# Start addresses of TensorE's operands: pads of 64 and 192 bytes

## The chip, the cores and the metric

The kernel runs on one NeuronCore of one Trainium2 chip. The core has TensorE (matrix products), VectorE (called DVE in the profile), ScalarE (ACT), GpSimd (POOL) and SyncE (SP, here only a queue that issues transfers). They share one on-chip memory of 128 partitions. A matrix product takes its two operands from that memory, one of them stationary (it is loaded into the array first, in the profile as PEld) and one moving (it streams past), and leaves its result in an accumulator memory. The metric is the device time of one execution in microseconds, lower is better.

## The reference

Four sequences of 3008 rows of 256 values go through a spectral layer and then, row by row, through a two-layer network:

```
X  = rfft(x, axis=1)                      # along the sequence
Yr = Xr @ w_r - Xi @ w_i + b_r            # complex 256 x 256 mix
Yi = Xr @ w_i + Xi @ w_r + b_i
Y  = soft-threshold(Yr, Yi; 0.01)
y  = irfft(Y, n=3008, axis=1)             # 12032 rows of 256
h  = y @ w_in                             # 256 -> 2048
out = (h * sigmoid(h)) @ w_out            # 2048 -> 256
```

All of it is float32.

## The kernel before

**The arithmetic.** The transforms are done as matrix products with tables (3008 = 47 x 64), in two stages forward (s1, s2), a mix per pair of frequencies, and two stages back (i1, i2). The network takes the result in 24 blocks of 512 rows. Most products are made of float32 values split into a high and a low part, each in the faster one-pass format (fp32r): three matmuls, high by high, high by low and low by high, add up in one accumulator. Such a matmul has 128 stationary columns and 256 moving ones. In this text it is called a split product. A few products are plain float32, which the array does in two passes, and they show as two records in the trace: the second forward stage (L344, L410), the last inverse stage (L544, L551), and parts of the first stage in the opening.

**The lines that matter.**

- L375 and L435: the mix of the first sequence and of the other three. Moving: the mix weights wr, wi, ws. Stationary: xh and xl.
- L482: the third stage, moving zh, zl; stationary the table t3.
- L620 (`mlp1`): the first layer for blocks 0 to 9 and the last. Moving: the block xt0 (high part), xt1 (low part). Stationary: the weights win0, win1. Twelve matmuls in a row a piece.
- L706 (`fast_product`): the first layer for blocks 10 to 22, in a form with seven products in place of eight. Moving: xt0, xt1 or sums made of them, th, tl. Stationary: win0, win1 or sums of them, sw_h0 to sw_h7 and sw_l0 to sw_l7.
- L777 (`mlp2`): the second layer. Moving: wout, high and low part 1024 bytes apart. Stationary: gh, gl, the activations.
- L551 and L544 (`i2`, `i2_ends`): they make the next block's 512 columns, in three pieces a block: `i2` with e = 0, `i2` with e = 1, and `i2_ends` (written "i2e" in the rows).

**What sets the order.** The order is written out by hand. A list of ticks, 16 for a block, says which twelve or so matmuls of the first layer run; between them stand the second-layer products of the tick before, and a table `fill` drops one piece of the spectral work into a tick. From tick 160 on (blocks 10 to 22, about 713 to 1277 us) the spectral work is over, and a tick holds only L706, L777 and, in three ticks of sixteen, a piece of L551 or L544.

**What sets the addresses.** Tiles lie in pools, each a stack in every partition, in the order in which they are asked for: cst at the bottom (tables, win, wout), then sb (the blocks xt, the tiles g, gh, gl, gin), then tf (all of the spectral work). When the spectral work ends, tf is given up and tl takes its place (th, tl, sw_h, sw_l, new gh and gl). A pad is a tile of [128, 16] float32 that nothing uses, which moves all tiles that come after it in its pool, and the pools above it, by 64 bytes:

```
    def shift(pool):

        state["shifts"] += 1
        pool.tile([128, 16], F32, bufs=1, name=f"shift{state['shifts']}")
```

There are seven pads: one in cst ahead of wout, one in sb, two in tf, and three in tl.

Of the kernel before, what the change touches and what calls it, by code (L numbers as in the profile page):

```python
# [9 lines left out]
F32 = mybir.dt.float32  # L10
F32R = mybir.dt.float32r
# [138 lines left out]
def spectral_mlp_kernel(ctx: ExitStack, tc: tile.TileContext, x, w_r, w_i, b_r, b_i, w_in, w_out, c1, c2, c3, c4, c3f, c5, out):  # L150
    nc = tc.nc
    cst = ctx.enter_context(tc.tile_pool(name="cst", bufs=1))
    sb = ctx.enter_context(tc.tile_pool(name="sb", bufs=2))
    tf = tc.alloc_tile_pool(name="tf", bufs=1)
    ps = ctx.enter_context(tc.tile_pool(name="ps", bufs=1, space=PSUM))
    dr = ctx.enter_context(tc.tile_pool(name="dr", bufs=1, space=DRAM))

    def shift(pool):

        state["shifts"] += 1  # L160
        pool.tile([128, 16], F32, bufs=1, name=f"shift{state['shifts']}")

    state = {"prologue": True, "fast": False, "d": 0, "xy": 0, "w": 0, "shifts": 0}
    c1_sb = tf.tile([128, 96], F32, name="c1_sb")
    c1_hl = [tf.tile([128, 96], F32R, name=f"c1_{i}") for i in range(2)]
    x_sb = [tf.tile([128, 4 * D], F32, name=f"x_sb{i}") for i in range(2)]
    c4_sb = cst.tile([120, 2 * (NP + RR)], F32, name="c4_sb")
    bias = tf.tile([128, 2, D], F32, name="bias")
# [1 line left out]
    wi = [tf.tile([128, 2, D], F32R, name=f"wi{i}") for i in range(2)]  # L170
    ws = [tf.tile([128, 2, D], F32R, name=f"ws{i}") for i in range(2)]
    win = [cst.tile([128, 2, DFF], F32R, name=f"win{i}") for i in range(2)]
    shift(cst)
    wout = cst.tile([128, NFF, 2, D], F32R, name="wout")
    scr1 = [dr.tile([NR, 128, D], F32, name=f"scr1_{b}") for b in range(NB)]
    scr2 = [dr.tile([NR, 128, D], F32, name=f"scr2_{b}") for b in range(NB)]

    tl = None
# [485 lines left out]
    def fast_moving(i):  # L664

        x32 = xf.pop(i)
        first = i == FAST[0]
        if first:
            shift(tl)
        d = tl.tile([128, 4, HB], F32, tag="td", bufs=1, name="td")  # L670
        hi = tl.tile([128, 4, HB], F32R, tag="th", bufs=2, name="th")
        lo = tl.tile([128, 4, HB], F32R, tag="tl", bufs=2, name="tl")
        if first:
            shift(tl)
        th[i] = (hi, lo)
        l0, r0, l1, r1 = x32[:, 0, 0:HB], x32[:, 0, HB:BLK], x32[:, 1, 0:HB], x32[:, 1, HB:BLK]

        def low(k):
            nc.gpsimd.tensor_sub(lo[:, k, :], d[:, k, :], hi[:, k, :])

        nc.gpsimd.tensor_sub(d[:, 0, :], r0, l0)
        yield
        nc.gpsimd.tensor_sub(d[:, 1, :], r1, d[:, 0, :])
        yield
        nc.gpsimd.tensor_sub(d[:, 2, :], r1, r0)
        nc.scalar.copy(hi[:, 0:2, :], d[:, 0:2, :])
        yield
        low(0)
        yield
        nc.gpsimd.tensor_sub(d[:, 3, :], l1, d[:, 1, :])  # L690
        yield
        low(1)
        nc.scalar.copy(hi[:, 2:4, :], d[:, 2:4, :])
        yield
        low(2)
        yield
        low(3)
# [160 lines left out]
    with tc.manual_schedule():  # L858
# [2 lines left out]
        nc.scalar.activation(out=first, in_=first, func=ACTF.Silu)  # L861
        zero = tf.tile([128, 512], F32, tag="c", bufs=1, name="zero")
        x_sb.append(tf.tile([128, 4 * D], F32, tag="sx", bufs=1, name="x_sb2"))
        shift(tf)
        c5_sb = tf.tile([128, 128], F32R, name="c5_sb")
        x_pre.extend(x_sb)
        x_pre.extend(sb.tile([128, 4 * D], F32, tag=f"xt{k}", bufs=1, name="x_pre") for k in ("a0", "a1", "b0", "b1"))
        shift(sb)
        nc.sync.dma_start(out=c1_sb, in_=c1)
        nc.gpsimd.memset(zero, 0.0)  # L870
        for n, t in enumerate(x_pre):
# [43 lines left out]
        def w_go(n=1):  # L915

            for _ in range(n):
                if w_run:
                    v = w_run[0]
                    v[0] += 1  # L920
                    if next(v[1], 0) == 0:
                        w_run.pop(0)
                    if v[0] == 2:
                        w_begin()
# [75 lines left out]
        g_load(0, 1, cols=slice(2 * D, 4 * D))  # L1000
        s1(1, 4, late=True)
        w_go()
        shift(tf)
        w_tags[:] = [(("zl", 2), ("zh", 2))]
        s1(1, 5, late=True)
        flush(2)
# [105 lines left out]
        for i in range(FAST[0], len(BLOCKS)):  # L1112
            if i in FAST:
                first = max(16 * i - 13, last + 1)
                t = last_stage(i, first)
                moving = fast_moving(i)
                for k in range(8):
                    at(t + 1 + (k if first == 16 * i - 13 else k // 2), next, moving, None)
                assert t + 8 < 16 * i or first > 16 * i - 13
            else:  # L1120
                last_stage(i, 16 * i - 7)

        def swap_pools():
            nonlocal tl
            tf.release()
            tl = ctx.enter_context(tc.tile_pool(name="tl", bufs=1, reuse_waits="tile"))
            shift(tl)

        fill.setdefault(last + 1, []).insert(0, (swap_pools, ()))
        for q in range(NFF // 2):  # L1130
            steps = fast_weights(q)
# [20 lines left out]
        for t in range(len(ticks) + 1):  # L1152
            i, f = ticks[t] if t < len(ticks) else (LAST, None)
# [38 lines left out]
        for k, (dst, src) in enumerate(stores):  # L1192
            eng = nc.scalar if k % 2 else nc.sync
            n = dst.shape[0]
# [27 lines left out]
```

## Time and profile before

| | |
|---|---|
| median of three runs | 1319.85 us (1319.2 to 1321.52) |
| the profiled execution, its own time | 1320.44 us |
| its span, first to last instruction | 1318.4 us |
| PE busy | 1305.7 us (99% of the span) |
| DVE, ACT, POOL busy | 902.6, 794.6, 196.8 us |
| mean granted TensorE clock | 0.999 of full speed |

PE is busy from the first products to the end. A matmul's record lasts longer than the distance to the next one, since matmuls overlap; what PE's work costs is read from the distance between the starts of two neighbours, called a step here. The timeline view merges equal neighbours into one row ("x12"), so the mean step of a group is the next row's start less its own, over the count.

### The profile page before, as it was taken

The numbers are of one execution on the slowest core, as the hardware profiler recorded it, in microseconds if no ns is written. First come the engines' busy times: TensorE is split into PE (matmuls) and PEld (weight loads), VectorE is DVE, ScalarE is ACT, GpSimd is POOL, SyncE is SP. The second block draws the span as 40 slices with busy tenths as digits, with TensorE's granted clock in tenths as the row PEclk, the third lists the DMA queues.
The fourth block names the chain that finished last, engine by engine and source line by source line (L and its number), as shares of the span: only waits on it lengthen the run. The fifth ranks groups of instructions, "written<-read, shape, count | busy, mean of one in ns | idle before, by whom it ended". The sixth has DMA issues, their size and how long they took to land.

```text
span 1318.4 us, 27508 instructions
## 1 busy us (share of the span) xinstructions
PE 1305.7 (99%) x10869; PEld 1279.3 (97%) x10869; DVE 902.6 (68%) x1723; ACT 794.6 (60%) x1664; POOL 196.8 (15%) x296
## 2 busy tenths in 40 slices
PE   8999999999999999999999999999999999999998
PEld 3989999999999999999999999999999999999998
DVE  3777747877767787566659666667666666666663
ACT  5556555767667666545555666656656665665554
POOL 2001002222122221121102110111011101100100
PEclk9999999999999999999999999999999999999999
DMA  8886324554365443433210111001001110110000
GB/s 267 269 250 192 115 64 116 130 152 104 108 183 138 122 137 82 134 94 111 69 62 12 38 32 32 6 28 32 23 8 40 33 32 2 32 32 16 2 23 25
DMA packets 76168, 110.30 MB, mean 84 GB/s; under 512 B 8880, under 2 KB 54824, under 8 KB 76040
## 3 DMA queue, kind: packets, MB, share of 16 engines
q1 hardware_dynamic: 61921, 79.17, 20.2%
q0 software_dynamic: 10544, 25.68, 7.7%
q10 hardware_dynamic: 3575, 3.70, 0.9%
q8 instruction: 86, 1.41, 0.4%
q14 instruction: 42, 0.34, 0.1%
HBM read 71.03 MB, written 37.49 MB: 82 GB/s over the span
## 4 chain that ended last, share of the span: by engine, by line
PE 96%; DMA 1%; DVE 1%; ACT 1%; issue 0%; POOL 0%; SPq 0%; DVEq 0%; ACTq 0%
PE acc L777 39%; PE h L706 19%; PE h L620 17%; PE mix L435 6%; PE mix L375 3%; PE s L410 2%; PE i L482 2%; PE i L551 2%; PE i2e L551 2%; PE s L304 1%; PE s L344 1%; DMA scr<-s1o 1%; PE s L266 1%; PE i L479 1%; PE i L544 1%; PE warm L886 0%
## 5 line engine op out<-in xcount | busy, mean ns | idle before, releaser
L777 PE MATMUL acc<-wout,gh 128*128 128x256 f32 x3008 | 550.5, 280 | 0.0
L777 PEld LDWEIGHTS acc<-wout,gh 128*128 128x128 f32 x3008 | 459.6, 188 | 3.5 <-issue 0.5
L777 PE MATMUL acc<-wout,gl 128*128 128x256 f32 x1504 | 419.2, 279 | 0.8 <-DVE gl L637 0.8
L777 PEld LDWEIGHTS acc<-wout,gl 128*128 128x128 f32 x1504 | 282.2, 188 | 1.4 <-DVE gl L637 1.4
L620 PE MATMUL h<-xt,win 128*128 128x256 f32 x2016 | 261.7, 278 | 0.4 <-ACT xt L579 0.3
L620 PEld LDWEIGHTS h<-xt,win 128*128 128x128 f32 x2016 | 243.8, 188 | 0.8 <-ACT xt L579 0.5
L627 ACT ACTIVATE g<-h 128x512 f32<-128x512 f32 (+1 forms) x177 | 101.8, 576 | 130.5 <-PE h L620 128.9
L754 DVE TENSOR_TENSOR gl<-gp,gh 128x512 fp32r<-128x512 f32 x208 | 148.5, 714 | 26.0 <-ACT gh L753 26.0
L744 ACT ACTIVATE gp<-gp 128x256 f32<-128x256 f32 x104 | 43.5, 418 | 177.0 <-DVE gp L741 177.0
L637 DVE TENSOR_TENSOR gl<-g,gh 128x512 fp32r<-128x512 f32 (+1 forms) x177 | 116.9, 661 | 47.7 <-ACT gh L636 46.0
L753 ACT CAST gh<-gp 128x512 fp32r<-128x512 f32 x208 | 129.0, 620 | 6.6
L706 PE MATMUL h<-xt,win 128*128 128x256 f32 x624 | 107.0, 279 | 0.0
L636 ACT CAST gh<-g 128x512 fp32r<-128x512 f32 (+1 forms) x177 | 106.2, 600 | 1.1 <-PE acc L777 0.3
L746 DVE TENSOR_TENSOR gp<-h,u 128x256 f32<-128x256 f32 x104 | 44.1, 424 | 78.6 <-ACT gp L745 78.6
L454 DVE TENSOR_TENSOR y<-q,mix 64x256 f32<-64x256 f32 x144 | 60.3, 419 | 45.0 <-PE mix L435 37.0
L706 PE MATMUL h<-th,sw_h 128*128 128x256 f32 x312 | 90.5, 290 | 0.0
L706 PEld LDWEIGHTS h<-xt,win 128*128 128x128 f32 x624 | 88.0, 188 | 0.0
L706 PE MATMUL h<-th,sw_l 128*128 128x256 f32 x312 | 87.1, 279 | 0.0
L706 PE MATMUL h<-tl,sw_h 128*128 128x256 f32 x312 | 86.7, 278 | 0.0
L741 DVE TENSOR_TENSOR gp<-h,u 128x256 f32<-128x256 f32 x104 | 44.1, 424 | 56.9 <-PE h L706 56.5
L442 POOL TENSOR_TENSOR q<-q,bias 128x256 f32<-128x256 f32 x36 | 29.0, 805 | 350.8 <-ACT q L441 350.8
L752 ACT ACTIVATE gp<-gp 128x512 f32<-128x512 f32 x104 | 66.1, 635 | 0.0
(167 smaller groups left out, 2333.9 us busy)
## 6 DMA issues: line engine op xcount, KB each, us to landing
a<-scr SPq DMA_DIRECT2D x48, 256.0 KB
x_sb<-in_x_dram POOLq DMA_DIRECT2D x64, 188.0 KB, 3.7
gin<-scr SPq DMA_DIRECT2D x48, 192.0 KB
t<-in_c_dram POOLq DMA_DIRECT2D x36, 256.0 KB, 3.6
scr<-i1o SPq DMA_DIRECT2D x36, 256.0 KB
t<-in_c_dram SPq DMA_DIRECT2D x48, 128.0 KB
scr<-s1o SPq DMA_DIRECT2D x32, 192.0 KB
scr<-s1o SPq DMA_DIRECT2D x13, 384.0 KB
```

What stands on the lines that cost most here:

```text
L435: nc.tensor.matmul(out=out, lhsT=x_[:, e, c, :], rhs=m[:, e, :], start=(n == 0), stop=(n == 5))
L454: nc.vector.tensor_tensor(out=y[64 * i:64 * i + 64, r, :], in0=q[rows, i, :], in1=pv[rows, i, :], op=op,)
L551: nc.tensor.matmul(out=p[:, o:o + NP + RR], lhsT=t[:, q:q + 128], rhs=c4_sb[:, h * (NP + RR):(h + 1) * (NP + RR)], start=(h == 0), stop=(h ...
L620: nc.tensor.matmul(out=p[:, c:c + D], lhsT=w[:, e, f * 128:(f + 1) * 128], rhs=v[:, e, c:c + D], start=(m == 0), stop=(m == 5),)
L627: nc.scalar.activation(out=g[:, q], in_=p[:, q], func=ACTF.Silu)
L636: nc.scalar.copy(gh[:, q], g[:, q])
L637: nc.vector.tensor_sub(gl[:, q], g[:, q], gh[:, q])
L706: nc.tensor.matmul(out=p, lhsT=w[j], rhs=m[k], start=(begins and n == 0), stop=(n == 2), skip_group_check=True,)
L752: nc.scalar.activation(out=v, in_=v, func=ACTF.Silu)
L753: nc.scalar.copy(h, v)
L754: nc.vector.tensor_sub(l, v, h)
L777: nc.tensor.matmul(out=a[:, 0:D], lhsT=v[:, q], rhs=wout[:, f, w, :], start=(begins and m == 0), stop=(ends and m == 2),)
```

## The change

`shift` gets the number of bytes as an argument. The pads in cst and sb stay at 64 bytes, one in tf stays at 64 and one (ahead of the tiles zl, zh) becomes 192; in tl the first stays at 64, the one ahead of td, th, tl becomes 192, the one behind them stays at 64. The small table c1, in two parts, gets its high part in cst, where it fills 384 bytes ahead of wout.

```
-    def shift(pool):
+    def shift(pool, n):
 
         state["shifts"] += 1
-        pool.tile([128, 16], F32, bufs=1, name=f"shift{state['shifts']}")
+        pool.tile([128, n // 4], F32, bufs=1, name=f"shift{state['shifts']}")
...
-    c1_hl = [tf.tile([128, 96], F32R, name=f"c1_{i}") for i in range(2)]
+    c1_lo = tf.tile([128, 96], F32R, name="c1_lo")
...
     win = [cst.tile([128, 2, DFF], F32R, name=f"win{i}") for i in range(2)]
-    shift(cst)
+    c1_hl = [cst.tile([128, 96], F32R, name="c1_hi"), c1_lo]
+    shift(cst, 64)
     wout = cst.tile([128, NFF, 2, D], F32R, name="wout")
...
         if first:
-            shift(tl)
+            shift(tl, 192)
         d = tl.tile([128, 4, HB], F32, tag="td", bufs=1, name="td")
         hi = tl.tile([128, 4, HB], F32R, tag="th", bufs=2, name="th")
         lo = tl.tile([128, 4, HB], F32R, tag="tl", bufs=2, name="tl")
         if first:
-            shift(tl)
+            shift(tl, 64)
...
-        shift(tf)
+        shift(tf, 64)
         c5_sb = tf.tile([128, 128], F32R, name="c5_sb")
...
-        shift(sb)
+        shift(sb, 64)
...
         w_go()
-        shift(tf)
+        shift(tf, 192)
         w_tags[:] = [(("zl", 2), ("zh", 2))]
...
             tl = ctx.enter_context(tc.tile_pool(name="tl", bufs=1, reuse_waits="tile"))
-            shift(tl)
+            shift(tl, 64)
```

The instructions of all five engines and their order stay as they are. Besides the addresses only some ten of the waits at the swap of tf for tl differ, as the new tiles lie over other old ones. Where the operands of the matmuls begin, modulo 256 bytes, before and after (every column slice that a matmul takes begins at a multiple of 256 bytes from its tile's start, but for the second half of c4):

| line | matmuls | moving | stationary |
|---|---|---|---|
| L375, L435 mix | 936 | 192, stays | 0, stays |
| L482 | 216 | 64 to 192 | 0, stays |
| L620 | 2016 | 64 to 192 | 0, stays |
| L706, moving xt | 819 | 64 to 192 | 0, stays |
| L706, moving xt, with sw_h0 to sw_l2 | 117 | 64 to 192 | 128 to 0 |
| L706, moving th or tl | 897 | 192, stays | 0, stays |
| L706, moving th or tl, with sw_h0 to sw_l2 | 351 | 192, stays | 128 to 0 |
| L777, blocks 10 to 22 (gh, gl in tl) | 2496 | 64 to 192 | 0, stays |
| L777, other blocks (gh, gl in sb) | 2016 | 64 to 192 | 128 to 0 |
| L304, 512 columns | 64 | 192, stays | 0, stays |
| L410, L344, two passes | 192 | 0, stays | 0, stays |
| L551, L544, two passes | 212 | 128 or 180, stay | 128 to 0 |

After the change every split product of 256 columns has 192 moving and 0 stationary.

## Rows read from the trace of the kernel before

**Rows 1.** The profile's page: span, and busy us (share) of the engines.

```profile
span 1318.4 us, 27508 instructions
PE 1305.7 (99%) x10869; PEld 1279.3 (97%) x10869; DVE 902.6 (68%) x1723; ACT 794.6 (60%) x1664; POOL 196.8 (15%) x296
```

**Rows 2.** Windows view: length; busy PE, PEld, DVE, ACT, POOL; PE clock; DMA.

```profile
720.00:1275.00 555.00, 555.00 (x4725) 555.00 (x4724) 376.64 (x780) 337.94 (x762) 72.55 (x96) 1.00 0.09 25
100.00:700.00 600.00, 599.07 (x5112) 594.28 (x5113) 429.07 (x762) 370.47 (x724) 112.64 (x178) 1.00 0.41 116
```

**Rows 3.** Windows view, counts by line: L777, L706, L551; then L777, L620, L435.

```profile
720.00:1275.00 555.00, 331.76 (x2403) 1.00 0.09 25
720.00:1275.00 555.00, 298.33 (x2106) 1.00 0.09 25
720.00:1275.00 555.00, 28.39 (x192) 25.32 (x192) 1.00 0.09 25
100.00:700.00 600.00, 238.64 (x1839) 1.00 0.41 116
100.00:700.00 600.00, 241.39 (x1869) 1.00 0.41 116
100.00:700.00 600.00, 82.28 (x648) 78.71 (x648) 1.00 0.41 116
```

**Rows 4.** Timeline of PE, 382 to 388 us: start, duration, engine, line.

```profile
382.30 0.40 PE L435 MATMUL mix<-wr,xh 128*128 128x256 f32 x2
...
384.43 0.40 PE L777 MATMUL acc<-wout,gh 128*128 128x256 f32 x2
...
385.81 1.52 PE L620 MATMUL h<-xt,win 128*128 128x256 f32 x12
387.17 0.63 PE L304 MATMUL s<-sx,c_sb 111*128 111x512 f32 x2
```

**Rows 5.** Timeline of PE, 1002 to 1005 us, blocks 10 to 22.

```profile
1002.49 0.40 PE L777 MATMUL acc<-wout,gh 128*128 128x256 f32 x2
...
1003.90 0.28 PE L706 MATMUL h<-th,sw_h 128*128 128x256 f32 x1
...
1004.25 0.28 PE L706 MATMUL h<-th,sw_h 128*128 128x256 f32 x1
...
1004.59 0.40 PE L777 MATMUL acc<-wout,gh 128*128 128x256 f32 x2
```

**Rows 6.** Timeline of PE, 35 to 38 us: L375 of the first pair.

```profile
35.59 0.39 PE L375 MATMUL mix<-wr,xh 128*128 128x256 f32 x2
...
37.63 0.60 PE L344 MATMUL s<-t,a 128*128 128x128 f32 x4
```

**Rows 7.** Timeline of PE, 390 to 395 us, behind L410.

```profile
390.37 1.05 PE L410 MATMUL s<-t,a 128*128 128x128 f32 x8
...
392.68 1.57 PE L620 MATMUL h<-xt,win 128*128 128x256 f32 x12
394.09 0.39 PE L777 MATMUL acc<-wout,gh 128*128 128x256 f32 x2
```

**Rows 8.** Timeline of PE: one block's three pieces of L551, then the next's.

```profile
808.42 0.65 PE L551 MATMUL i<-c_sb,gin 120*128 120x141 f32 x4
814.19 0.65 PE L551 MATMUL i<-c_sb,gin 120*128 120x141 f32 x4
819.98 1.13 PE L551 MATMUL i2e<-c_sb,gin 120*128 120x141 f32 x8
820.85 0.38 PE L706 MATMUL h<-th,sw_h 128*128 128x256 f32 x1
852.62 1.13 PE L551 MATMUL i<-c_sb,gin 120*128 120x141 f32 x8
```

**Rows 9.** Lines view, one fifth matmul behind i2e, then behind i2.

```profile
L706 PE MATMUL h<-th,sw_l 128*128 128x256 f32 x1 | 0.3, 276 | 0.0
L706 PE MATMUL h<-th,sw_l 128*128 128x256 f32 x1 | 0.3, 281 | 0.0
```

## The prediction

> **What bounds the kernel now.** I read the page's head first: PE is busy for 1305.7 of 1318.4 us, the next engine, DVE, for 902.6 [rows 1]. Then the windows view for the two long stages. In blocks 10 to 22 (720 to 1275 us) PE is busy for all of 555.00 us, with DVE at 376.64 and ACT at 337.94; in the spectral stage (100 to 700 us) for 599.07 of 600, with DVE at 429.07. The column behind them, the granted clock, is 1.00 in both [rows 2]. So PE sets the time, no engine behind it is near its own limit, and the clock does not explain differences in PE's pace. What is left is the step from one matmul to the next.
>
> The timeline shows two steps for one and the same form of matmul. Twelve L620 take 387.17 - 385.81 = 1.36 us, 113.3 ns each; just ahead, eighteen L435 take 384.43 - 382.30 = 2.13 us, 118.3 ns each [rows 4]. In blocks 10 to 22 twelve L777 take 1003.90 - 1002.49 = 1.41 us, 117.5 ns [rows 5]. L620 itself, fast at 385.81, takes 394.09 - 392.68 = 1.41 us for twelve, 117.5 ns, at another place [rows 7]. There is no third pace: 113.3 and about 118 ns, some 4.5 ns apart. Which one a run of matmuls has is decided at its head and then stays. That is what the change can act on: it alters no instruction, only where operands begin.
>
> **How much is there.** In 720 to 1275 us stand 2403 + 2106 = 4509 split products [rows 3]. The 192 records of L551 come in groups of 8; one lasts 820.85 - 819.98 = 0.87 us [rows 8], and I add 0.09 for the slow first step behind it: 24 x 0.96 = 23 us. L544's few and their changeovers I put at 3. (555 - 26) / 4509 = 117.3 ns a step: this stage runs at the slow pace nearly throughout. At 113.3 it would save 4509 x 4.0 = 18.0 us.
> In 100 to 700 us stand 1839 + 1869 + 648 split products [rows 3] and 216 of L482, 4572. The two-pass products and L304 I put at 70 us, from groups like the eight L410 that begin at 390.37 and L551's [rows 7, 8]. (600 - 70) / 4572 = 115.9 ns: a mixture of both paces, with at most 2.6 x 4572 = 12 us to be had. The opening and the last 40 us hold another 1 us. The ceiling of the change is so 18 + 12 + 1 = 31 us.
>
> **What decides the pace.** I sorted the timeline's steps by the starts in the table of the change, as the distance of stationary from moving modulo 256.
>
> - Distance 192 (64 and 0, or 192 and 128): whatever pace comes in stays. L620 keeps it for twelve matmuls at either pace [rows 4, 7].
> - Distance 64 (64 and 128, or 192 and 0): the slow pace often ends within five steps. L706 with 192 and 0 takes 1004.25 - 1003.90 = 0.35 us for its first three matmuls and 1004.59 - 1004.25 = 0.34 for the next, which is 113.3 ns [rows 5]. I found no run at this distance that went from fast to slow while the starts stayed the same, but for two or three steps in more than a thousand.
> - A switch of the starts between neighbours throws the pace over. The L620 that ends at 382.30 is fast, and L435 behind it (moving from 64 to 192) is slow from its first step; L706 has just become fast at 1004.59, and L777 behind it (192 to 64) is slow again [rows 4, 5]. In blocks 10 to 22 such a switch comes every six to twelve matmuls, between L777 or xt (64) and th, tl (192): this is why the stage is slow.
>
> After the change all split products have 192 and 0, at distance 64, and no switch is left between them. What remains are the changes to and from two-pass products. Then the pace should be set behind each of these, and stay until the next.
>
> The Trainium skill speaks against this. "TensorE: Matmul & The Clock Gate", Part 2 (What happens when you issue a matmul), first step, says that the moving operand and the weight load have two independent read ports, so that loading the next weights takes nothing from the running matmul. By that rule the starts of the two could not matter to each other, and the sum would be zero. The trace doesn't agree: one form runs at 113.3 and at 118 ns at the same granted clock [rows 2, 4, 7].
>
> **The sum, blocks 10 to 22.** A block has three pieces of L551 or L544. In the one shown they begin at 808.42, 814.19 and 819.98, and the next block's at 852.62 [rows 8]: stretches of 5.8, 5.8 and 32.6 us of 44.2.
> - Behind the third (i2e) comes L706 with 192 and 0 already now, and the fifth matmul lasts 276 ns, the mark of the fast pace, against 281 behind the second piece [rows 9]. So it is in all 12 blocks of this stage. Today L777 ends it six matmuls later. I take this stretch as fast.
> - Behind the second, also 192 and 0 now, 4 of 12 become fast. I take it as slow for two thirds.
> - Behind the first stands 192 and 128 now, so no row shows the new case. Bounds: all fast, all slow; I take half.
> Slow: (5.8 x 0.67 + 5.8 x 0.5) / 44.2 = 15%. The gain is 18.0 x 0.85 = 15.3 us; with the first and second piece fast 18, and with the third slow too 0 or less.
>
> **The sum, the spectral stage.** Two edits pull against each other. Switches that begin a stretch at 118 ns go: L435 takes over L620's pace (648 x 4.6 = 3.0 us if always fast; that 192 and 0 in the mix can be fast is shown by L375 at 35.59, eighteen in 2.04 us, 113.3 ns [rows 6]). But switches that end such a stretch go too. Behind L410 L777 starts slow, L620 stays slow until 394.09, where the next switch makes L777 fast [rows 7]. This is so behind nearly all 36 groups of L410, and without a switch it would last to the next two-pass or L304 product. The first edit is worth 3 us by its own count and the second about as much with the sign turned (36 stretches, two pieces longer each, 24 steps of 4.5 ns, are 4 us). I take 0, with bounds +10 (all slow: 4572 x 2.1) and -12 (all fast).
>
> **The other edits** cost nothing that a row shows: the two-pass products' stationary tiles move from 128 to 0, c1's high part into cst, and transfers land 384 bytes further on. Fifteen matmuls of L243 stand in the opening, behind transfers. I take 0, bounded by 1 us either way, the whole of the opening's excess. What PE's pace asks of the others: DVE's 376.64 us in a stage of 540 instead of 555 is 70%, less than the 72% it has in the spectral stage [rows 2], so no new wait of size.
>
> Together: 1320.44 - 15.3 = 1305.1 us for an execution like the profiled one; the median of the runs lies 0.6 below that one, so 1304.5.
>
> **Rivals.**
> 1. *192 and 0 locks the slow pace.* L435 stands at just these starts and never becomes fast in eighteen matmuls [rows 4]; behind L410 the same distance locks too [rows 7]. If this held behind i2e also, once gh and wout follow L706, every step would be 118: 4509 x 0.7 = 3 us more in blocks 10 to 22, 10 us more in the spectral stage, together 1333. It decides from the point where more than nine tenths of blocks 10 to 22 stay slow. Against it: the fifth matmul behind i2e, and L375's eighteen matmuls at 113.3 ns with the same starts [rows 6, 9]. 12%.
> 2. *The starts are not the cause.* The pace would then follow from something that goes with the stage, such as the form of the loop or the engines' writes, and the change would only shuffle it: 1319.9, give or take 1. The Trainium skill's rule on the two ports, above, would have it so. Against it: L706 becomes fast and slow within one tick as its starts go from 64 to 192 and back [rows 5]. 9%.
> 3. *All fast.* If the first and second piece behave like i2e, and the entries of the spectral stage too, the ceiling is reached: 1320 - 31 = 1289. Half of it in the spectral stage gives 1295. It is the forecast's lower edge; 14%.
>
> **How the numbers follow.** The forecast (blocks 10 to 22 mostly fast, the spectral stage between -9 and +6) has 65%; with it and the third rival, faster has 0.79. Rival 1 gives slower, 0.12. Rival 2 gives no change, 0.09; about 0.2% is what a measurement of this kernel can tell from none. The range reaches from 1293, where the forecast meets the third rival, to 1318, a gain of 2 us, where blocks 10 to 22 gain a third of the ceiling and the spectral stage loses 4. It leaves out rival 1, rival 2 and the far end of rival 3.
>
> **What would show it.** Right: behind i2e, L777 and L706 at 113.3 ns for the whole 32 us, so that the 4509 split products fill about 511 us instead of 529; L435 as fast as the L620 ahead of it; 276 ns, the mark of the fast pace, as the duration of most L777 there. Stretches at 118 ns begin at a two-pass or L304 product and nowhere else. Wrong: L777 still at 118 behind L706, a switch of pace where the starts stay the same, or a new idle time of PE in front of gl or gh.

## The result, and the profile after

| | before | after |
|---|---|---|
| median, both run again on one chip | 1320.68 us (1319.2 to 1323.96, 4 runs) | 1308.72 us (1308.18 to 1309.91, 4 runs) |
| ratio | 1 | 0.9907, 95% interval 0.9887 to 0.9928 |
| span of the profiled execution | 1318.4 us | 1306.3 us |

The change makes the kernel 12.0 us faster; 1304.5 was predicted, with a range of 1293 to 1318. Lines behind L172 have numbers one higher than before: L778 is L777 of before, L707 is L706, L621 is L620, L436 is L435, L411 is L410, L552 is L551.

The page's head after answers to [rows 1]: PE is still busy 99% of the span.

```profile
span 1306.3 us, 27506 instructions
PE 1292.0 (99%) x10869; PEld 1264.1 (97%) x10869; DVE 897.0 (69%) x1723; ACT 795.5 (61%) x1664; POOL 196.8 (15%) x296
```

The windows view of the stretches of [rows 2] (window and length; busy PE and matmuls; granted clock, DMA share, GB/s):

```profile
100.00:700.00 600.00, 598.78 (x5082) 1.00 0.42 115
720.00:1275.00 555.00, 555.00 (x4854) 1.00 0.09 25
```

Equal windows hold another number of matmuls: in blocks 10 to 22, 4854 instead of 4725, in the spectral stage 5082 instead of 5112. One stage gained, the other lost, at the same granted clock of 1.00.

The timeline at the L777 and L706 of [rows 5], now:

```profile
998.81 0.39 PE L778 MATMUL acc<-wout,gh 128*128 128x256 f32 x2
...
1000.17 0.28 PE L707 MATMUL h<-th,sw_h 128*128 128x256 f32 x1
...
1000.51 0.28 PE L707 MATMUL h<-th,sw_h 128*128 128x256 f32 x1
...
1000.85 0.39 PE L778 MATMUL acc<-wout,gh 128*128 128x256 f32 x2
```

Twelve L778 take 1.36 us, 113.3 ns each (117.5 before), and six L707 behind them 0.68, the same. The place of [rows 4], now:

```profile
385.45 0.39 PE L436 MATMUL mix<-wr,xh 128*128 128x256 f32 x2
...
387.49 0.39 PE L778 MATMUL acc<-wout,gh 128*128 128x256 f32 x2
...
388.85 1.52 PE L621 MATMUL h<-xt,win 128*128 128x256 f32 x12
390.21 0.40 PE L305 MATMUL s<-sx,c_sb 111*128 111x512 f32 x1
```

Eighteen L436 take 2.04 us: 113.3 ns, as the L621 ahead of them. The other face of it, at 570 us of the spectral stage, behind an L411 as in [rows 7]:

```profile
569.85 1.05 PE L411 MATMUL s<-t,a 128*128 128x128 f32 x8
...
572.15 1.58 PE L621 MATMUL h<-xt,win 128*128 128x256 f32 x12
573.56 0.40 PE L436 MATMUL mix<-wr,xh 128*128 128x256 f32 x2
...
575.68 0.40 PE L778 MATMUL acc<-wout,gh 128*128 128x256 f32 x2
...
577.10 1.58 PE L621 MATMUL h<-xt,win 128*128 128x256 f32 x12
578.51 0.50 PE L411 MATMUL s<-t,a 128*128 128x128 f32 x3
```

From 572.15 to 578.51 stand 54 products in 6.36 us, 117.8 ns each, through three changes of line, up to the next L411. With the same starts everywhere nothing ends a stretch that began badly.

Blocks 10 to 22: the three pieces of the block of [rows 8], as the two-pass products and what follows them.

```profile
810.63 0.38 PE L707 MATMUL h<-th,sw_h 128*128 128x256 f32 x1
...
814.61 0.40 PE L778 MATMUL acc<-wout,gh 128*128 128x256 f32 x2
...
816.03 0.65 PE L552 MATMUL i<-c_sb,gin 120*128 120x141 f32 x4
816.42 0.38 PE L707 MATMUL h<-th,sw_h 128*128 128x256 f32 x1
...
817.21 0.39 PE L778 MATMUL acc<-wout,gh 128*128 128x256 f32 x2
...
817.89 0.28 PE L707 MATMUL h<-xt,sw_h 128*128 128x256 f32 x1
...
821.63 1.13 PE L552 MATMUL i2e<-c_sb,gin 120*128 120x141 f32 x8
822.50 0.38 PE L707 MATMUL h<-th,sw_h 128*128 128x256 f32 x1
...
823.98 0.28 PE L707 MATMUL h<-xt,sw_h 128*128 128x256 f32 x1
...
825.00 0.39 PE L778 MATMUL acc<-wout,gh 128*128 128x256 f32 x2
```

The first piece stays at 118 to its end (twelve L778 from 814.61 to 816.03: 118.3 ns). The second is at 113.3 from 817.21 on (six in 0.68), the third likewise (nine from 823.98 to 825.00 in 1.02). Sorting all 39 stretches between two-pass products by the step of each matmul: the first piece is at 118 throughout in 8 of the 12 blocks, the second in none, the third in 1 of 12 (at 735.4, 31 us). Behind the fifth matmul of a stretch the pace stays to its end, but where PE pauses. In the first of the 39 it does so twice: behind a step of 518 ns at 716.9 us, a wait for gl, the pace is 113 as before it; behind one of 219 ns at 721.7 us it is 118. So a pause too can set the pace anew. In the whole kernel 148 of 151 stretches are at one pace behind their fifth matmul, and the other three hold pauses.

All kernels here issue the same 10869 matmuls in the same order, so their profiled executions, one of each kernel, can be cut at the same matmuls. "Opening" ends at the start of the 601st, blocks 10 to 22 reach from the first L706 to the last; us:

| kernel | opening | spectral | blocks 10 to 22 | rest |
|---|---|---|---|---|
| before | 108.4 | 604.5 | 573.6 | 31.9 |
| after | 108.0 | 608.1 | 558.4 | 31.8 |
| e1_undo_th | 108.2 | 608.6 | 575.3 | 32.7 |
| e2_far192 | 107.5 | 606.4 | 573.4 | 31.7 |
| e3_one_pad | 106.8 | 604.7 | 557.1 | 31.7 |
| e4_mix64 | 111.1 | 602.1 | 556.9 | 31.5 |
| e5_win128 | 107.1 | 604.9 | 556.8 | 31.6 |
| e6_low64 | 109.5 | 618.5 | 573.6 | 32.5 |
| e7_same0 | 107.7 | 624.3 | 585.2 | 33.1 |
| e8_opp128 | 110.4 | 613.4 | 581.2 | 32.3 |
| e9_gl0 | 108.1 | 600.8 | 556.6 | 31.3 |

So the 12.1 us of the span are 15.2 gained in blocks 10 to 22, 3.6 lost in the spectral stage, and 0.5 elsewhere. The opening, which waits for transfers, lies between 106.8 and 111.1 us in these single executions; whether the starts have a part in that, the runs don't show.

### The profile page after: what moved, and what is told of

Its sections match the earlier page's. It is cut to its first block, busy times and chain, and to the rows that moved or that the text cites. A ratio compares the mean times of both kernels' runs of the same rounds, so it can differ in the third digit from the quotient of the medians.

```text
span 1306.3 us, 27506 instructions
## 1 busy us (share of the span) xinstructions
PE 1292.0 (99%) x10869; PEld 1264.1 (97%) x10869; DVE 897.0 (69%) x1723; ACT 795.5 (61%) x1664; POOL 196.8 (15%) x296
## 3 DMA queue, kind: packets, MB, share of 16 engines
q8 instruction: 86, 1.41, 0.4%
## 4 chain that ended last, share of the span: by engine, by line
PE 93%; DMA 3%; DVE 2%; ACT 1%; issue 0%; POOL 0%; SPq 0%; ACTq 0%; DVEq 0%
PE acc L778 39%; PE h L707 19%; PE h L621 17%; PE mix L436 6%; PE s L411 2%; PE i L483 2%; PE mix L376 2%; PE i L552 2%; PE i2e L552 1%; PE s L305 1%; DMA scr<-s1o 1%; PE s L267 1%; PE i L480 1%; PE s L345 1%; DMA t3f<-in_c3f_dram 1%; PE i L545 1%
## 5 line engine op out<-in xcount | busy, mean ns | idle before, releaser
L778 PE MATMUL acc<-wout,gh 128*128 128x256 f32 x3008 | 543.6, 278 | 0.0
L778 PEld LDWEIGHTS acc<-wout,gh 128*128 128x128 f32 x3008 | 458.2, 188 | 3.5 <-issue 1.0
L778 PE MATMUL acc<-wout,gl 128*128 128x256 f32 x1504 | 417.7, 278 | 0.9 <-DVE gl L638 0.9
L778 PEld LDWEIGHTS acc<-wout,gl 128*128 128x128 f32 x1504 | 282.7, 188 | 1.5 <-DVE gl L638 1.5
L621 PE MATMUL h<-xt,win 128*128 128x256 f32 x2016 | 264.5, 280 | 0.4 <-ACT xt L580 0.3
L621 PEld LDWEIGHTS h<-xt,win 128*128 128x128 f32 x2016 | 246.3, 188 | 0.8 <-ACT xt L580 0.5
L707 PE MATMUL h<-xt,win 128*128 128x256 f32 x624 | 105.0, 277 | 0.0
L707 PE MATMUL h<-th,sw_h 128*128 128x256 f32 x312 | 90.1, 289 | 0.0
L707 PE MATMUL h<-th,sw_l 128*128 128x256 f32 x312 | 86.6, 277 | 0.0
L707 PEld LDWEIGHTS h<-xt,win 128*128 128x128 f32 x624 | 86.5, 188 | 0.0
L707 PE MATMUL h<-tl,sw_h 128*128 128x256 f32 x312 | 86.4, 277 | 0.0
```

The lines of the kernel that those rows point to most:

```text
L621: nc.tensor.matmul(out=p[:, c:c + D], lhsT=w[:, e, f * 128:(f + 1) * 128], rhs=v[:, e, c:c + D], start=(m == 0), stop=(m == 5),)
L707: nc.tensor.matmul(out=p, lhsT=w[j], rhs=m[k], start=(begins and n == 0), stop=(n == 2), skip_group_check=True,)
L778: nc.tensor.matmul(out=a[:, 0:D], lhsT=v[:, q], rhs=wout[:, f, w, :], start=(begins and m == 0), stop=(ends and m == 2),)
```

## The experiments

Starts are written moving/stationary, modulo 256; "distance" is stationary minus moving, also modulo 256. All edits are widths of pads (one of 0 bytes is left out) or places of tiles; the work is complete in each kernel.

**e1_undo_th: the whole change, but th and tl keep another moving start than the rest.** Against after:

```
         if first:
-            shift(tl, 192)
+            shift(tl, 64)
         d = tl.tile([128, 4, HB], F32, tag="td", bufs=1, name="td")
...
         if first:
-            shift(tl, 64)
+            shift(tl, 192)
```

> The changed kernel with one part undone: th and tl begin at 64 in place of 192 (the pad ahead of them 64, the one behind 192); all else as after the change (wout, xt at 192, stationary at 0). Theory A (a switch of the moving start between neighbours throws the pace to 118 ns, and with no switch it stays): blocks 10 to 22 hold a switch every six to twelve matmuls again, their 4509 split products go back to 117 ns or more, and the time is 1308.7 + 15 = about 1323 us. Theory B (only the distance of 64 between the starts of neighbours counts, each matmul for itself): the 3261 products with 192 and 0 stay at 113.3 to 114 ns, only the 1248 with th and tl go to 118, and the time is 1308.7 + 5 = about 1313 us. Theory C (starts are not the cause): no change, 1308.7.

Measured 1326.23 us (1324.44 to 1327.48, 6 runs), ratio to before 1.0036 (1.0024 to 1.0048). The timeline where L778 (192/0) meets L707 with th (64/0):

```profile
1007.21 0.39 PE L778 MATMUL acc<-wout,gh 128*128 128x256 f32 x2
...
1008.62 0.28 PE L707 MATMUL h<-th,sw_h 128*128 128x256 f32 x1
...
1009.33 0.40 PE L778 MATMUL acc<-wout,gh 128*128 128x256 f32 x2
```

Twelve L778 in 1.41 and six L707 in 0.71: 118 ns. The two moving starts alone take back all 15.2 us, and 1.7 more. Theory A, that a switch of the moving start throws the pace to 118, stands (about 1323 us expected); B (1313) and C (1308.7) fall.

**e3_one_pad: one number of before altered.** All moving tiles of blocks 10 to 22 then begin at 64, all stationary ones but win at 128; the spectral stage is left alone.

```
         if first:
-            shift(tl)
+            shift(tl, 192)
         d = tl.tile([128, 4, HB], F32, tag="td", bufs=1, name="td")
```

> The kernel before with one number altered: the pad ahead of td, th, tl is 192 bytes in place of 64. In blocks 10 to 22 all moving tiles then begin at 64 (xt, wout, th, tl); stationary ones at 128 (sw, gh, gl), but for win at 0. The spectral stage is as before. Theory A in the form that only a switch of the moving start does harm: the stationary start still changes between 0 and 128, as it does between L620 and L777 in the spectral stage, where such a change ended stretches at 118 ns; blocks 10 to 22 go to about 113.6 ns, and as the spectral stage loses nothing the time is 1320 - 16.5 = 1303.5 us, below the changed kernel. Theory A' (any switch of a start does harm): the stage stays near 117 ns, 1320 us. Theory D (moving must begin at 192): 1320 us.

Measured 1303.34 us (1301.79 to 1304.99, 4 runs), ratio 0.9865 (0.9847 to 0.9883): some 5 us faster than the change, with the width of one pad altered, and as expected. Its timeline at the same L777 as above (numbers three higher than before):

```profile
993.09 0.39 PE L780 MATMUL acc<-wout,gh 128*128 128x256 f32 x2
...
994.45 0.28 PE L709 MATMUL h<-th,sw_h 128*128 128x256 f32 x1
...
995.13 0.39 PE L780 MATMUL acc<-wout,gh 128*128 128x256 f32 x2
```

Twelve in 1.36, six in 0.68. The table has the rest: blocks 10 to 22 at 557.1 us, 1.3 below after, and the spectral stage as before. So blocks 10 to 22 gain with the one moving start at 64 as well: 192 is not special. The pad also moves gh, gl and most of sw from 0 to 128, so e3 alone doesn't show that the missing switch is enough, and e2 shows that it isn't.

**e2_far192: one moving start, but distance 192 throughout (64/0 in blocks 10 to 22).** Against before, again the two pads in tl:

```
         if first:
-            shift(tl)
+            shift(tl, 64)
         d = tl.tile([128, 4, HB], F32, tag="td", bufs=1, name="td")
...
         if first:
-            shift(tl)
+            shift(tl, 192)
...
             tl = ctx.enter_context(tc.tile_pool(name="tl", bufs=1, reuse_waits="tile"))
-            shift(tl)
+            shift(tl, 192)
```

> The kernel before with the three pads of tl alone altered (192, 64, 192): in blocks 10 to 22 every split product has moving 64 and stationary 0, one distance (192) and no switch; the spectral stage is the same as before, address by address. Theory A: without a switch the pace set behind each two-pass product stays; L620 at these starts came out at 113.3 ns behind most i2e pieces, so the long stretch of a block runs at 113.3 and the mean of the stage is about 114.3: 1320 - 13 = 1307 us. Theory B (the distance must be 64): the stage stays at 117.3 ns, 1320 us. Theory D (moving must begin at 192): 1320 us too.

Ten runs fell in two groups, with nothing between: three at 1302.69 to 1302.77 and seven at 1320.08 to 1322.46; median 1320.54, ratio 0.9945 (0.9901 to 0.9989), which says little of two groups. The profiled one is of the second group:

```profile
1003.16 0.40 PE L780 MATMUL acc<-wout,gh 128*128 128x256 f32 x2
...
1004.58 0.28 PE L709 MATMUL h<-th,sw_h 128*128 128x256 f32 x1
```

118.3 ns, although no start of a split product changes by 128 within blocks 10 to 22. In it 89% of the 4620 products of blocks 10 to 22 are at 118 ns, all twelve third pieces among them; at 4.6 ns each that is 18.9 us, and the groups lie 18.3 apart (1321.0 - 1302.7). An estimate, then: in the other group nearly all of them are at 113. Theory A's mixture near 1307 didn't come, and none of the three theories foresaw two times. A missing switch alone is not enough: it keeps a bad pace too. What decides between the two from one execution to the next, these runs don't show; no execution of the first group was profiled.

**e6_low64: one moving start and distance 64, as after, but at 64/128 in blocks 10 to 22.** Against before (the name behind # is the tile that follows the pad):

```
+    shift(cst, 128)   # win
-    shift(cst)        # wout
+    shift(cst, 192)
-            shift(tl) # td
+            shift(tl, 192)
-        shift(tf)     # c5_sb
-        shift(sb)
...
-            shift(tl) # first tile of tl
+            shift(tl, 128)
```

> Uniform starts in blocks 10 to 22 with the same distance of 64 as after the change, but 128 bytes lower: moving 64, stationary 128, win too. The spectral stage has other starts than either kernel (L620 64 and 128, L777 64 and 64, mix 128 and 128) and is not compared. If only the distance counts, and not where the operands begin, blocks 10 to 22 take 556 to 560 us from their first to their last first-layer product, as after the change (558.4); if moving must begin at 192 they take 573 as before.

Measured 1336.18 us (1336.0 to 1338.24, 3 runs), ratio 1.0118 (1.0101 to 1.0134). Behind i2e:

```profile
835.65 1.13 PE L554 MATMUL i2e<-c_sb,gin 120*128 120x141 f32 x8
...
837.33 0.40 PE L780 MATMUL acc<-wout,gh 128*128 128x256 f32 x2
...
838.04 0.28 PE L709 MATMUL h<-xt,sw_h 128*128 128x256 f32 x1
```

Six L780 in 0.71 us, 118.3 ns, where after has 113.3. Only 7 stretches of the 39, all of them behind L544 of before or right after one, reach 113. So the distance alone does not choose the pace: it allows both, and which comes is set at the entry behind the two-pass product. Blocks 10 to 22 take 573.6 us, not the 556 to 560 of a distance that decides by itself. The other reading of the expectation, that moving must begin at 192, gives about this time, but falls with e3 (moving at 64, 557.1 us). Two more things differ from after and are not separated here: the stationary tile of the two-pass L551 and L544 begins at 64 instead of 0, and modulo 512 the stationary tiles of the split products lie at two starts (3234 products at 128, 1404 at 384), where after has 4194 of 4662 at one. The second holds for e2 as well (3234 at 0, 1404 at 256).

**e7_same0 and e8_opp128: distance 0 everywhere (0/0), and distance 128 in blocks 10 to 22 (128/0).** Against before, e7 first:

```
+    shift(tf, 192)    # c1
-    shift(cst)        # wout
-            shift(tl) # td, and the one behind tl
-        shift(tf)     # c5_sb
-        shift(sb)
-        shift(tf)     # zl
```

```
-    shift(cst)        # wout
+    shift(cst, 128)
-            shift(tl) # td, the one behind tl, and the first of tl
+            shift(tl, 128)
```

> All split products begin at 0 with both operands: distance 0, no switch. If a missing switch is all that is needed, blocks 10 to 22 keep the pace that is set behind each two-pass piece, and take between 555 us (all at 113.3 ns) and 575 (all at 118), perhaps one or the other from execution to execution as e2 did. If the two operands of one start get in each other's way, every product is at 118 ns or above, and the stage takes 576 us or more.

> In blocks 10 to 22 moving tiles begin at 128 and stationary ones at 0: distance 128, no switch (the spectral stage has a mixture: L620 128 and 0, L777 128 and 192, mix 0 and 64). Same two outcomes as for distance 0: between 555 and 575 us for the stage if a missing switch is what counts, at or above 576 if this distance locks 118 ns. With the distances 0, 64, 128 and 192 all measured, it shows whether 64 is the one that falls to 113.3 ns by itself.

Measured 1352.36 us (1351.76 to 1354.59, 3 runs), ratio 1.0239 (1.0222 to 1.0256), and 1339.36 us (1336.7 to 1339.51, 3 runs), ratio 1.0131 (1.0114 to 1.0147). The same twelve L777, in e7 and then in e8:

```profile
1027.33 0.40 PE L780 MATMUL acc<-wout,gh 128*128 128x256 f32 x2
...
1028.77 0.28 PE L709 MATMUL h<-th,sw_h 128*128 128x256 f32 x1
```

```profile
1016.84 0.40 PE L780 MATMUL acc<-wout,gh 128*128 128x256 f32 x2
...
1018.27 0.28 PE L709 MATMUL h<-th,sw_h 128*128 128x256 f32 x1
```

1.44 and 1.43 us: 120.0 and 119.2 ns. These are paces of their own: in blocks 10 to 22 nine of ten steps of e7 are at 120, and those of e8 go round between 115 and 123, with a mean of 119.1. Neither shows 113.3 ns for long. The stage takes 585.2 and 581.2 us, over the 576 that the expectations set for distances that hold every product at 118 or above.

**e5_win128: after, with only win moved, to 128.** L621 is then at distance 192 and all others at 64: the moving start never changes, the stationary one does.

```
-    win = [cst.tile([128, 2, DFF], F32R, name=f"win{i}") for i in range(2)]
     c1_hl = [cst.tile([128, 96], F32R, name="c1_hi"), c1_lo]
+    win = [cst.tile([128, 2, DFF], F32R, name=f"win{i}") for i in range(2)]
```

> The changed kernel with one tile placed otherwise: c1's high part lies ahead of win in place of behind it, so win begins at 128 modulo 256 and nothing else moves (all moving tiles at 192, other stationary ones at 0). Between L620 and L777, and between the products with win and with sw or gh in blocks 10 to 22, the stationary start now changes by 128, as it did in the kernel before and does in e3. Theory A'' (such a change of the stationary start alone ends stretches at 118 ns, and its loss is why the spectral stage lost 3 us by the change): the spectral stage gets back 4 to 6 us, blocks 10 to 22 another 2, and the time is 1308.7 - 6.5 = about 1302 us. Theory A' (any switch of a start does harm, the stationary one too): slower than 1308.7, up to 1320. Theory G (the loss of the spectral stage comes from gh at 0 or xt at 192, not from the missing change): 1308.7 us.

Measured 1302.91 us (1302.43 to 1304.18, 4 runs), ratio 0.9864 (0.9848 to 0.9881). Behind an L411:

```profile
389.89 1.05 PE L411 MATMUL s<-t,a 128*128 128x128 f32 x8
...
392.20 1.57 PE L621 MATMUL h<-xt,win 128*128 128x256 f32 x12
393.61 0.39 PE L778 MATMUL acc<-wout,gh 128*128 128x256 f32 x2
...
394.97 1.30 PE L621 MATMUL h<-xt,win 128*128 128x256 f32 x10
```

Twelve L621 in 1.41 us (117.5), and the twelve L778 behind them in 1.36 (113.3). Of 56 such changes from 192/128 to 192/0 that a stretch at 118 met, 55 ended it; of the 176 the other way that one at 113 met, 175 left it at 113. It works as a ratchet, with few exceptions: from distance 192 to 64 the pace improves or stays, and back it stays. The spectral stage takes 604.9 instead of 608.1 us, 3.2 less where 4 to 6 were expected, and blocks 10 to 22 take 1.6 less. Theory A'' stands; A' and G, with no time below 1308.7, fall.

**e4_mix64: e3, with wr, wi and ws at a moving start of 64, as all else.**

```
-    c1_hl = [tf.tile([128, 96], F32R, name=f"c1_{i}") for i in range(2)]
+    c1_hl = [None, tf.tile([128, 96], F32R, name="c1_lo")]
...
     ws = [tf.tile([128, 2, D], F32R, name=f"ws{i}") for i in range(2)]
+    c1_hl[0] = tf.tile([128, 96], F32R, name="c1_hi")
```

> e3 with one more move: the small table c1's high part is asked for behind ws in place of ahead of the mix weights, so that wr, wi, ws begin at 64 as xt and wout do (xh, xl stay at 0). Theory A: L435 no longer begins with a switch from 64 to 192, takes over L620's pace, 113.3 ns in most of its 36 places, and the 648 products of L435 save up to 3.0 us: 1303.5 - 2.5 = 1301 us. Theory E (the mix is at 118 ns for another reason, such as its tiles lying in one region): L435 stays at 118 ns and the time is that of e3.

Measured 1302.19 us (1301.3 to 1303.54, 4 runs), ratio 0.9854 (0.9839 to 0.9869). The mixing of [rows 4], now:

```profile
384.56 0.39 PE L439 MATMUL mix<-wr,xh 128*128 128x256 f32 x2
...
386.60 0.39 PE L781 MATMUL acc<-wout,gh 128*128 128x256 f32 x2
```

Eighteen L439 take 2.04 us, 113.3 ns; so do 576 of the 648. Theory E falls. The spectral stage takes 602.1 us, 2.6 less than in e3. In the profiled execution the opening is 4.3 us longer and hides that; the medians differ by 1.2 us, and the ranges of the two kernels overlap.

**e9_gl0: e4, with gl at 0 and gh still at 128.** Each triple of the last product then has a change of the stationary start from 128 to 0 and back, with the moving start at 64. The stationary tile of the two-pass L551 and L544 moves from 128 to 0 along with it.

```
-            h, l = [tl.tile([128, 2, HB], F32R, tag=f"g{k}", bufs=4, name=f"g{k}") for k in "hl"]
+            h = tl.tile([128, 2, HB], F32R, tag="gh", bufs=4, name="gh")
+            if (i, q, r) == (FAST[0], 0, 0):
+                shift(tl, 128)
+            l = tl.tile([128, 2, HB], F32R, tag="gl", bufs=4, name="gl")
...
+        sb.tile([128, 512], F32, tag="g", bufs=3, name="g_first")
+        sb.tile([128, 512], F32R, tag="gh", bufs=3, name="gh_first")
+        c1_hl[0] = sb.tile([128, 96], F32R, bufs=1, name="c1_hi")
```

> As the kernel in which every moving tile begins at 64 (mixing too), but the low part gl now begins at 0 while the high part gh stays at 128: each triple of L777 products (gh, gh, gl) changes its stationary start from 128 to 0 and back, all else stays. Theory (a change of the stationary start alone, from distance 192 to 64, ends a stretch at 118 ns, and the change back does no harm): blocks 10 to 22 keep under 5% of their split products at 118 ns, and in the spectral stage the excess of L777 over 113.33 ns falls from 2.0 to under 1 us and that of L620 from 1.7 to under 1; together some 2 to 3 us less, about 1299.5 us. Rival (any change of the start of either operand can throw the pace over): L777 mostly at 118 ns in blocks 10 to 22, 10 us slower or more than the kernel it comes from, 1312 to 1320 us. Third reading (what is left there belongs to the first steps behind two-pass products and no change of start reaches it): 1302, no change.

Measured 1297.94 us (1297.76 to 1300.52, 5 runs), ratio 0.9829 (0.9815 to 0.9842): the fastest version here. The same place behind L410 of before, in e4 and then in e9:

```profile
392.54 1.05 PE L414 MATMUL s<-t,a 128*128 128x128 f32 x8
...
394.50 0.40 PE L781 MATMUL acc<-wout,gh 128*128 128x256 f32 x2
394.73 0.28 PE L781 MATMUL acc<-wout,gl 128*128 128x256 f32 x1
394.85 1.57 PE L624 MATMUL h<-xt,win 128*128 128x256 f32 x12
396.26 0.39 PE L781 MATMUL acc<-wout,gh 128*128 128x256 f32 x2
```

```profile
388.67 1.05 PE L414 MATMUL s<-t,a 128*128 128x128 f32 x8
...
390.61 0.39 PE L784 MATMUL acc<-wout,gh 128*128 128x256 f32 x2
390.83 0.28 PE L784 MATMUL acc<-wout,gl 128*128 128x256 f32 x1
390.95 1.52 PE L624 MATMUL h<-xt,win 128*128 128x256 f32 x12
392.31 0.39 PE L784 MATMUL acc<-wout,gh 128*128 128x256 f32 x2
```

In e4 the twelve L624 still go at 117.5 (1.41 us), in e9 at 113.3 (1.36): the bad stretch ended at the first change from gl back to gh. The rival, that a change inside each triple does harm, falls with blocks 10 to 22 at 556.6. But the size came by another way than expected. Excess over 113.33 ns, summed over the spectral steps, fell for L624 from 1.65 to 0.77 us, as expected, and rose for the last product (L777 of before) from 1.96 to 2.78 instead of falling below 1. Where the last product stands right behind L410 (9 places of 36) its first twelve lose 21 ns instead of 56, but behind L304 42 instead of 22, and behind L482 26 instead of 12: more of these entries begin at 118 before the ratchet acts. All in all the two stages gain 1.3 + 0.3 us on e4; the other 3 us between the two profiled executions are the opening (108.1 against 111.1), so of the 4.2 us between the medians only about 1.6 is shown to come from the starts.

## Why the prediction was right

**The cause: right.** That starts act on the pace, and that a switch of the moving start ends the fast one, is shown by e1 (put it back: 575.3 us) and by the steps: over before, e1 and e3, each of the 111 runs at 113 ns that met such a switch went on at 118 (counted where six or more matmuls stand on either side). Rival 2 (the starts are not the cause) falls: one form of matmul ran at 113.3, 118, about 119 and 120 ns with operands that begin at other places, at a granted clock of 1.00 and with the same order of instructions. The Trainium skill's rule in "TensorE: Matmul & The Clock Gate", Part 2 (What happens when you issue a matmul), first step, that loading the next weights takes nothing from the running matmul, is not borne out here: with the start of the weights win alone altered (e5) the spectral stage takes 604.9 us instead of 608.1. Rival 1 (192/0 locks the slow pace) falls too: 192/0 keeps whichever pace it is given. "There is no third pace" holds only for the starts of before: e7 and e8 have 120 and 119. And a switch does not always do the same: the change from 64/0 to 192/0 ended 38 of 39 stretches at 118 in before (L777 to L706), but 1 of 103 in e1 (L707 to L778). By the tiles' addresses that 64 is 320 modulo 512 in before and 64 in e1, so starts modulo 256 may not be the whole of it.

**Blocks 10 to 22: the sum right, its pieces not.** Predicted 15.3 us, measured 15.2; predicted 15% of the products at 118, measured about 700 of 4620, 15%. But the step "fast at the third, two thirds slow at the second, half slow at the first" was wrong in its parts: the second piece is at 113 in all 12 blocks, the first at 118 in 8, and one third piece of 31 us stays at 118. The errors cancelled, so that the size came out this close is luck. So it is with the 26 us of the two-pass products: L551's groups are of 8 records in half the cases and of 4 in the others, which is less (22.3 us with L544), but the slow first steps cost more (3.6), 25.9 in all. The mark "about 511 us" for 4509 products goes with all of them fast; the sum itself makes it 513.7, and the mean step in after, 114.05 ns, makes it 514.3. e6 shows how little that share was known: at the same distance, with 64/128 for 192/0, nearly every stretch lands at 118.

**The spectral stage: mis-sized.** The term was 0, with bounds of +10 and -12; it measured +3.6 us. The first half of the balance was half of what was counted: L436 went from all at 118 to half of them (its excess from 3.0 to 1.4 us), since it takes over the pace of what is ahead of it, and that is not always 113. The second half was larger than counted. It was worked out as 36 stretches behind L410, two pieces longer each, from one place [rows 7]. Only 9 of the 36 have L777 right behind them, as there; behind the other 27 stands L482. After the change 16 of the 36 stay at 118 to their end (before: 6); behind L305 20 of 32 stay at 118 to their end (before: 7), and the two behind L285, with 432 products from 119.6 us on, are at 118 throughout (before: at 113), which alone is 432 x 4.6 = 2.0 us. I counted one kind of entry and left out the others. What ended such stretches in before was not just any switch, as the prediction had it, but the change of the stationary start at a fixed moving one (64/0 to 64/128, from L482 or L620 to L777), as e5 shows; each of the 36 changes from L435 to L777, with both starts moving (192/0 to 64/128), left the pace at 118. With win's start alone altered 3.2 of the 3.6 us come back: 1.4 in L436, some 1.9 in the long stretch of 408 products, and the entries of the other lines about cancel. The 12 us that were the most to be had here were too many too: over before's steps from 100 to 700 us the excess above 113.33 ns is 8.3 us, since the two-pass products, L304 and the steps behind them take 82 of the 600 us in place of 70.

**The other edits: right within what can be told.** No new wait of size appeared: PE is busy 555.00 of 555 us in blocks 10 to 22, and DVE is at 69%. The predicted mark, stretches at 118 that begin at two-pass or L304 products alone, holds in after but for the pause at 721.7 us, and 276 ns is the duration of most L778 there (2131 of 2478).

Together: predicted -15.3 + 0, measured -15.2 + 3.6 and -0.5 elsewhere, 3.2 of the 4.2 us between forecast and result. Most of the rest is the start of the sum: it set out from a median of 1319.85 us, and run again with after the same kernel had 1320.68.

## What to carry to other kernels

When an engine is busy all the time at full clock and one form of matmul still shows two steps, look at where its two operands begin in their partition before looking for work to remove: give all moving tiles one start, keep it off the stationary tiles' start and off 128 bytes from it (e7, e8), and change the pads one at a time. Uniform starts take away what makes a run slow but also what would make it fast again; a stationary start that alternates at a fixed moving start got both here (1297.94 us). Measure such a version in several executions, since a pace that is set at an entry and then kept can differ from one to the next (e2).

## What the runs showed of the hardware

- The step of a one-pass 128x256 product goes with the starts of its operands. Sorted modulo 256 bytes it is 113.3 or 118 ns at distances 64 and 192, 120 at 0 (e7) and 119.1 on average at 128 (e8). That 256 is the right period is not shown: in blocks 10 to 22 of every kernel but e7, moving starts that are equal modulo 256 are equal modulo 512 too.
- At 64 and 192 both paces last: the pace is set within about five matmuls behind a two-pass product, a 512-column one or a pause, and then kept as long as the starts stay: in after through a stretch of 408 products at 118 and through one of 405 at 113.
- At one moving start, a change of the stationary start from distance 192 to 64 ended 154 of 157 stretches at 118 (e3, e4, e5), and the change back left 618 of 621 at 113. A change of the moving start by 128 did the opposite: none of 111 stretches at 113 outlived it (before, e1, e3).
- One kernel had two times, 1302.7 and 1320 to 1322 us, from execution to execution, at a granted clock of 0.997 to 1.0 in all ten (e2). Why the entries fall as they do, and by what means the two starts meet, no run here shows.
